# Forgetting attention with FFN: weight loading begins at the third pair, six pairs normalised behind the values

## The chip, the cores and the metric

One core of a Trainium2 chip runs the whole program in one launch. The metric is the device time of one execution in microseconds (us), the median of several runs. The engines of the core work side by side and meet at semaphores: PE (TensorE, matmuls and transposes), PEld (PE's weight loads, which overlap its matmuls), DVE (VectorE), ACT (ScalarE), POOL (GpSimd) and SP (SyncE, which issues most DMAs). Each engine takes its instructions strictly in the order in which the built program has them.

## The reference

Attention with a decay, causal, for 8 x 8 heads of 576 tokens and 64 channels, then a two-layer FFN over the 4608 tokens:

```python
scores = scale * q @ k.T                            # per head, scale = 1/8
cum = cumsum(log(clip(f, 1e-4, 1)))
scores = where(causal, -1e9, scores + cum[i] - cum[j])
attn = exp(scores - max)
attn = attn / (sum(attn) + 1e-9)
x = attn @ v                                        # heads side by side: 4608 x 512
h = x @ w_in                                        # 512 x 2048
out = maximum(0.01 * h, h) @ w_out                  # 2048 x 512
```

All inputs and outputs are fp32. The weights are handed to the kernel as the int64 words of their values and are turned into fp32 on the chip.

## The kernel before

**Accuracy.** The large matmuls run in fp32r. An operand x is split into a rounded high part and the rest, x = xh + xl, and a product is made of three matmuls: high by high, low by high, high by low. A smaller matmul may run in fp32; then one matmul of the program is two instructions on PE, except a transpose, which is one.

**The early stage.** The first 256 tokens of three batches (NE = 3) are computed by a short path, two heads (a *pair*) at a time: 12 pairs in a list `steps`. For each pair
- `early_scores` makes the scores on PE (tiles `sce`, from `qk` and from the decay in `both`), takes the row minimum on DVE (L340), the exponential and the row sum on ACT (L344), and one over the sum on DVE (L347, L348). Then the four blocks of exponentials, `ze`, are multiplied by it: on DVE (L351) in the first SCALED = 4 pairs, on ACT (L353) in the others;
- `early_values` transposes `ze` on PE (`tre`), copies the transposes on ACT (`pte`, L365), multiplies with the values on PE (`ave`, two heads into the lower and the upper 64 partitions of one tile), and evicts the result: as high and low parts `xh` (ACT, L378) and `xl` (DVE, L379) where an FFN group of 256 tokens takes it directly (batches 0 and 1), else by a copy to DRAM (L374).

**The weights.** 16 pieces of 1 MB, w_in and w_out in turn, two for each of the eight p (256 of the 2048 hidden channels). `load_weight` turns a piece into fp32 and splits it. The first SUMMED = 5 pieces let PE add up the low part (`ws`, L118; three matmuls for each of two halves, evicted at L212); the others make it on DVE alone (L195, L214, L215, L218, L219). All begin with an activation on ACT (L189) and make the high part on ACT (L200). The raw words lie in two buffers in turn (RAWS), so the load of piece n + 2 waits until piece n is turned. The first two loads are on SP's queue, the others on POOL's (L173).

**The FFN.** `ffn()` is a generator; a step of it is a *quantum*. For a group n of 256 tokens and one p it makes `h` (24 matmuls over 256 columns), g, gh and gl (ACT and DVE), and `o` (12 matmuls over 512 columns), in four quanta. The order is: group 0 and then group 1 with p = 0 to HP - 1 (HP = 4), kept as partial sums; then both with the other p; then the groups from 2 on, and two wide blocks of 512 tokens at the end. A quantum is not given out while its weights or its tokens aren't there; what the call had to spend then falls away.

**What sets the order.** Three tuples with an entry for each pair: after the scores of pair x, pieces are loaded up to the sum of WQ[:x + 1]; after the values of pair x - 1, `fill(FQ[x])` gives out that many quanta. `warm(n)` issues n matmuls on zeros, whose result isn't used, at the start (WARM[0] = 14) and behind the scores of the first pair (WARM[1] = 8). A scheduler then orders each engine's instructions; the order shown below is its result. After the 12 pairs the main stage runs 64 heads with the full-length path (`sc`, `tr`, `av`), with quanta between them, and what is left of the FFN follows.

Of the kernel before, what the change touches and what calls it, by code (L numbers as in the profile page):

```python
# [8 lines left out]
F32 = mybir.dt.float32  # L9
# [4 lines left out]
ALU = mybir.AluOpType  # L14

P = 128
DELAY = 90
ORDER = (0, 3, 4, 5, 6, 7, 1, 2)
HP = 4
PARTS = (("part0", 1), ("part1", 1), ("ost", 2), ("ost", 2))  # L20
MAXQ = 9
AT = 2
# [5 lines left out]
B2 = 5  # L28
B4 = 4
NE = 3  # L30
WQ = (1, 1, 1, 1, 1, 1, 1, 1, 2, 2, 2, 2)
ZE = (("z0", "z1", "z2", "z3"), ("e0", "e1", "e2", "e3"))
FQ = (0, 0, 0, 0, 4, 8, 8, 8, 8, 8, 8, 4, 2)
BUFS = dict(s1=2, m1=2, ost=2)
RAWS = ("ph", "pl")
WARM = (14, 8)
SCALED = 4
SUMMED = 5
NEG = -1.0e30
REBIAS = 2.0**-112  # L40
SIGN = -(2.0**32)
# [3 lines left out]
def forgetting_attention_ffn(ctx, tc, qT, kT, v4, vr, f, w_in, w_out, out):  # L45
# [6 lines left out]
    nc = tc.nc  # L52
    NHEAD, D, S = qT.shape
# [3 lines left out]
    HPB = NHEAD // NB  # L57
# [5 lines left out]
    T = 256  # L63
# [12 lines left out]
    def width(i):  # L76
        return min((i + 1) * P, S)
# [23 lines left out]
    one = ctx.enter_context(tc.tile_pool(name="one", bufs=1))  # L101
# [14 lines left out]
    def matmul(*args, **kw):  # L116
        work[0] += 1
        nc.tensor.matmul(*args, **kw)  # L118

    def transpose(*args):  # L120
        work[0] += 1
        nc.tensor.transpose(*args)  # L122
# [3 lines left out]
    def warm(n):  # L126

        ps = psum.tile([P, 512], F32, tag="h", name=f"warm_{len(warmed)}", bufs=1)
        warmed.append(n)
        for x in range(n):  # L130
            last = nc.tensor.matmul(ps, still[:, :P], still, start=True, stop=True)
            if x == 0 and len(warmed) > 1:
                tc.keep_in_program_order(last)

    warm(WARM[0])
    eye = one.tile([P, P], F32, tag="part0", name="eye")
# [3 lines left out]
    ident = ident_r.bitcast(F32)  # L140
# [36 lines left out]
    def load_weight(n):  # L177
# [12 lines left out]
        if n == 0:  # L190
            tc.keep_in_program_order(first)
        if n < SUMMED:
            first = nc.vector.tensor_scalar(t, t, 3, None, op0=ALU.logical_shift_left)
# [6 lines left out]
        nc.scalar.copy(wh, tf)  # L200
        if n < SUMMED:
            nc.vector.tensor_scalar(hi, t, -0x800000, None, op0=ALU.bitwise_and)
# [74 lines left out]
    def load(t):  # L277

        s, c0, c1 = tasks[t]
        h = state[t] = {}  # L280
        a, n = c0 * P, S
        x = h["raw"] = one.tile([P, S], F32, tag="qraw", name=f"raw_{t}")
        for y, src in ((x[:D, a:n], qT[s][:, a:n]), (x[D:, :n], kT[s][:, :n])):
            last = nc.sync.dma_start(y, src)
            if t < 2:
                tc.keep_in_program_order(last)
        if s % 2 == 0:
            pairs[s // 2, c0] = {}

    def load_v(t):  # L290

        g, o = tasks[t][0] // 2, tasks[t][0] % 2
        vm = fixed["vm"]
        for y, src in ((vm[:, :NFULL], v4[g][:, o]), (vm[:REST, NFULL], vr[g][:, o])):
            last = nc.sync.dma_start(y, src)
            if t < 1:
                tc.keep_in_program_order(last)
# [3 lines left out]
    def early_load(b, g):  # L301

        e = early[b, g] = {}
        x = e["qk"] = one.tile([P, 2, T], F32, tag="m1", name=f"qk_{b}_{g}", bufs=2)
        for y, src in enumerate((qT, kT)):
            nc.sync.dma_start(
                x[:, y], src[b * HPB + 2 * g:b * HPB + 2 * g + 2, :, :T].rearrange("s d n -> (s d) n")
            )

    def early_load_v(b, g):  # L310

        v = early[b, g]["v"] = one.tile([P, 2, T // P, D], F32, tag="b2", name=f"ve_{b}_{g}", bufs=B2)
        nc.sync.dma_start(v, v4[b * HPB // 2 + g][:, :, :T // P])

    def early_scores(b, g):
        e = early[b, g]
        mx = one.tile([P, 4], F32, tag="max", name=f"maxe_{b}_{g}", bufs=3)
        sm = one.tile([P, 4], F32, tag="sum", name=f"sume_{b}_{g}", bufs=3)
        for i in range(2):
            n = width(i)  # L320
            ps = [
                psum.tile([P, 512], F32, tag="sc", name=f"sce_{b}_{g}_{2 * o + i}")[:, :n]
                for o in range(2)
            ]
            for o in range(2):
                x = e["qk"][o * D:(o + 1) * D]
                matmul(ps[o], x[:, 0, i * P:n], x[:, 1, :n], start=True, stop=False)
            for o in range(2):
                s = b * HPB + 2 * g + o
                matmul(  # L330
                    ps[o], pick[:, s:s + 1].broadcast_to([P, P]), decay_r[i],
                    start=False, stop=True,
                )
            for o in range(2):
                c = 2 * o + i
                tag = ZE[g % 2][c]
                z = e[c] = one.tile(
                    [P, n], F32, tag=tag, name=f"ze_{b}_{g}_{c}", bufs=BUFS.get(tag, 1)
                )
                nc.vector.tensor_tensor_reduce(  # L340
                    out=z, in0=ps[o], in1=tri[:, TRI - n:], scale=-SCALE, scalar=3.0e38,
                    op0=ALU.add, op1=ALU.min, accum_out=mx[:, c:c + 1],
                )
                nc.scalar.activation(  # L344
                    z, z, AF.Exp, bias=mx[:, c:c + 1], scale=-1.0, accum_out=sm[:, c:c + 1]
                )
        nc.vector.tensor_scalar(sm, sm, 1.0e-9, None, op0=ALU.add)  # L347
        nc.vector.reciprocal(sm, sm)  # L348
        for c in range(4):
            if b * HPB // 2 + g < SCALED:  # L350
                nc.vector.tensor_scalar(e[c], e[c], sm[:, c:c + 1], None, op0=ALU.mult)  # L351
            else:
                nc.scalar.activation(e[c], e[c], AF.Copy, scale=sm[:, c:c + 1])  # L353

    def early_values(b, g):
        e = early[b, g]
        pts = []
        for o in range(2):
            ps = psum.tile([P, 512], F32, tag="tr", name=f"tre_{b}_{g}_{o}")
            for x, (c, j) in enumerate(((2 * o, 0), (2 * o + 1, 0), (2 * o + 1, 1))):  # L360
                transpose(
                    ps[:, x * P:(x + 1) * P], e[c][:, j * P:(j + 1) * P], ident
                )
            pt = one.tile([P, 3 * P], F32, tag=("z4", "e4")[o], name=f"pte_{b}_{g}_{o}")
            nc.scalar.copy(pt, ps[:, :3 * P])  # L365
            pts.append(pt)
        out = psum.tile([P, 512], F32, tag="tr", name=f"ave_{b}_{g}")
        for o, pt in enumerate(pts):
            rows_ = slice(o * D, (o + 1) * D)
            matmul(out[rows_, :T], e["v"][:, o, 0], pt[:, :T], start=True, stop=False)  # L370
            matmul(out[rows_, P:T], e["v"][:, o, 1], pt[:, T:], start=False, stop=True)
        if b not in groups:
            x = one.tile([P, T], F32, tag="x", name=f"xe_{b}_{g}")
            nc.scalar.copy(x, out[:, :T])  # L374
            nc.sync.dma_start(xd[g * P:(g + 1) * P, b * T:(b + 1) * T], x)
            return
        xh, xl = groups[b]
        nc.scalar.copy(xh[:, g, :], out[:, :T])  # L378
        nc.vector.tensor_tensor(xl[:, g, :], out[:, :T], xh[:, g, :].bitcast(F32), op=ALU.subtract)  # L379

    fixed = {}

# [231 lines left out]
    groups, staged = {}, {}  # L614
# [25 lines left out]
    def ffn():  # L640
        pending = None
        half = NFC // 2
        order = [(0, 0, HP), (1, 0, HP), (0, HP, half), (1, HP, half)]
        order += [(n, 0, half) for n in range(2, NG - 2 * WIDE)]
# [184 lines left out]
    for n in range(2):  # L829
# [8 lines left out]
        out=tri[:, TRI - P:], in_=tri[:, TRI - P:], pattern=[[-1, P]], base=0, channel_multiplier=1,  # L838
# [11 lines left out]
    for x, (b, g) in enumerate(steps + [(NE, 0)]):  # L850
        if 2 <= x + 1 < len(steps):
            early_load(*steps[x + 1])
            early_load_v(*steps[x + 1])
        if x < len(steps):
            early_scores(b, g)
            if x == 0:
                warm(WARM[1])
            if x in (8, 11):
                load(x // 11)
            if x == 8:  # L860
                load_v(0)
            if x == 10:
                split(0)
            weights(sum(WQ[:x + 1]))
        if x == 6:
            decay_rows()
        if x:
            early_values(*steps[x - 1])
            if steps[x - 1][1] == HPB // 2 - 1:
                ready[0] = (steps[x - 1][0] + 1) * T  # L870
        if x == len(steps):
            fixed["vs"] = one.tile([P, 2, NCH, 2 * D], F32R, tag="vs", name="fixed_vs")
            split_v(0)
            load_v(1)
            split(1)
        fill(FQ[x])
    fix_z()
# [73 lines left out]
```

## Time and profile before

| | |
|---|---|
| median of 3 runs | 1202.01 us (1201.11 to 1202.22) |
| the profiled execution's own time | 1203.28 us |
| its span, first to last instruction | 1201.3 us |
| PE busy | 1185.2 us, 7422 matmuls |
| DVE, ACT, POOL busy | 597.5, 630.3, 432.1 us |
| granted clock of PE, mean | 0.999 |
| read from HBM, written | 65.32 MB, 18.58 MB |

The span is a little shorter than the execution's time, since the launch lies around it. A group of instructions is named by its line in the kernel, its engine, its operation and `out<-in` with the tiles' names; the line is that of a helper where one issues them all (L118 for every matmul, L122 for every transpose). Busy time of PE is modelled: a matmul's row lasts until its end, while the next has begun long before. What a matmul costs is therefore read from where the next one starts, or from a run of several in the chain of waits. Such a run counts hardware instructions.

### The profile page before, as it was taken

To read this page: it belongs to the slowest core of one execution; us is meant where nothing else is said; L and a number is where in the kernel's file an instruction comes from. 1 tells how busy PE (TensorE), PEld (TensorE's weight loads), DVE (VectorE), ACT (ScalarE), POOL (GpSimd) and SP (SyncE) were. 2 spreads that over 40 slices of the span, in tenths; PEclk is the share of its full clock that TensorE was granted. 3 is DMA by queue.
4 is the path that set the end of the run, shared out by engine and by line. 5 is a ranking of instruction groups with operands and counts; after the bars stand their busy time and mean duration, and the time that the engine had idled before them with its cause. 6 is when DMAs were issued, how large, how long until landed. Compare 5 with 4: busy or idle time off the path is not lost.

```text
span 1201.3 us, 21523 instructions
## 1 busy us (share of the span) xinstructions
PE 1185.2 (99%) x7422; PEld 1043.4 (87%) x7422; DVE 597.5 (50%) x1695; ACT 630.3 (52%) x1629; POOL 432.1 (36%) x476
## 2 busy tenths in 40 slices
PE   8999999999999999999999999999999999999998
PEld 5777888989989899989999999999999998888886
DVE  7888365566555554455445545454435553221121
ACT  6776565677665555555555565555555652111111
POOL 3111254545554445454545444444545520000000
PEclk9999999999999999999999999999999999999999
DMA  6565233344343233333333332323232322000001
GB/s 222 172 211 167 73 102 96 100 117 119 106 143 85 78 96 104 111 81 92 109 96 90 110 97 77 111 77 94 59 104 71 88 73 77 1 1 20 16 1 36
DMA packets 81229, 110.49 MB, mean 92 GB/s; under 512 B 20640, under 2 KB 49936, under 8 KB 81120
## 3 DMA queue, kind: packets, MB, share of 16 engines
q1 hardware_dynamic: 76864, 94.16, 27.5%
q0 software_dynamic: 4032, 14.68, 3.6%
q8 instruction: 59, 0.97, 0.3%
q14 instruction: 50, 0.41, 0.1%
q10 hardware_dynamic: 224, 0.28, 0.1%
HBM read 65.32 MB, written 18.58 MB: 70 GB/s over the span
## 4 chain that ended last, share of the span: by engine, by line
PE 88%; DVE 4%; DMA 3%; ACT 2%; issue 2%; POOL 1%; SPq 0%; DVEq 0%; ACTq 0%; POOLq 0%
PE h L118 24%; PE o L118 23%; PE ow L118 7%; PE hw L118 7%; PE av L118 7%; PE tr L122 7%; PE sc L118 7%; PE sce L118 2%; PE ws L118 1%; PE ave L118 1%; DVE fixed_z L451 1%; DVE x L604 1%; DVE gh L684 1%; ACT g L681 1%; DVE pl L511 1%
## 5 line engine op out<-in xcount | busy, mean ns | idle before, releaser
L457 ACT ACTIVATE fixed_z<-fixed_z,max 128x192 f32<-128x192 f32 (+3 forms) x272 | 160.9, 592 | 101.5 <-DVE max L451 98.4
L686 POOL TENSOR_TENSOR gl<-g,gh 128x512 fp32r<-128x512 f32 x95 | 124.8, 1314 | 198.3 <-DVE gh L684 193.9
L509 ACT CAST ph<-tr 128x192 fp32r<-128x192 f32 (+3 forms) x360 | 126.0, 372 | 106.1 <-PE tr L122 74.2
L118 PE MATMUL o<-wout_h,gh 128*128 128x512 f32 x448 | 179.9, 402 | 0.3 <-ACT part L799 0.3
L118 PE MATMUL o<-wout_h,gl 128*128 128x512 f32 x448 | 176.7, 394 | 0.0
L118 PE MATMUL o<-wout_l,gh 128*128 128x512 f32 x448 | 176.5, 394 | 0.0
L451 DVE CUSTOM_DVE_ANT_0 fixed_z<-sc,tri 128x192 f32<-128x192 f32 (+3 forms) x272 | 120.9, 450 | 99.9 <-PE sc L118 98.2
L511 DVE TENSOR_TENSOR pl<-tr,ph 128x384 fp32r<-128x384 f32 (+3 forms) x296 | 136.9, 467 | 66.9 <-ACT ph L509 63.1
L118 PE MATMUL h<-xh,win_h 128*128 128x256 f32 x896 | 164.3, 287 | 0.0
L118 PE MATMUL h<-xh,win_l 128*128 128x256 f32 x896 | 159.1, 282 | 0.0
L122 PE MATMUL tr<-ident_r,fixed_z 128*128 128x128 f32 x888 | 144.0, 273 | 1.7 <-DVE x L571 1.2
L118 PEld LDWEIGHTS h<-xh,win_h 128*128 128x128 f32 x896 | 133.6, 190 | 3.9 <-issue 0.5
L118 PEld LDWEIGHTS h<-xh,win_l 128*128 128x128 f32 x896 | 129.6, 190 | 0.2
L118 PE MATMUL sc<-m,s 128*128 128x288 f32 (+1 forms) x336 | 123.0, 369 | 4.5 <-DVE max L451 4.1
L122 PEld LDWEIGHTS tr<-ident_r,fixed_z 128*128 128x128 f32 x888 | 108.0, 140 | 18.2 <-issue 1.7
L118 PE MATMUL h<-xs,win_h 128*128 128x256 f32 x768 | 123.3, 283 | 0.0
L684 DVE CAST gh<-g 128x512 fp32r<-128x512 f32 x112 | 54.3, 485 | 119.3 <-ACT g L681 113.6
L118 PEld LDWEIGHTS h<-xs,win_h 128*128 128x128 f32 x768 | 105.7, 192 | 0.0
L118 PEld LDWEIGHTS o<-wout_h,gl 128*128 128x128 f32 x448 | 84.2, 188 | 18.9 <-issue 0.2
L681 ACT ACTIVATE g<-h 128x512 f32<-128x512 f32 x112 | 66.3, 592 | 62.9 <-PE h L118 56.4
L719 ACT ACTIVATE gw<-hw 128x512 f32<-128x512 f32 x32 | 19.1, 597 | 150.9 <-PE hw L118 150.9
L118 PEld LDWEIGHTS o<-wout_h,gh 128*128 128x128 f32 x448 | 84.6, 189 | 12.8 <-ACT part L799 0.5
(152 smaller groups left out, 2151.6 us busy)
## 6 DMA issues: line engine op xcount, KB each, us to landing
raw<-in_kT SPq DMA_DIRECT2D x64, 144.0 KB
m<-m SPq DMA_DIRECT2D x64, 144.0 KB
fixed_vm<-in_v SPq DMA_DIRECT2D x64, 128.0 KB
wraw<-in_w_in POOLq DMA_DIRECT2D x14, 512.0 KB, 4.4
wraw<-in_w_out POOLq DMA_DIRECT2D x14, 512.0 KB, 4.3
xs<-xd SPq DMA_DIRECT2D x12, 512.0 KB
raw<-in_qT SPq DMA_DIRECT2D x40, 144.0 KB
s<-s SPq DMA_DIRECT2D x40, 144.0 KB
```

Source lines behind the costliest of these rows:

```text
L118: nc.tensor.matmul(*args, **kw)
L122: nc.tensor.transpose(*args)
L451: nc.vector.tensor_tensor_reduce(out=z[:, a:b], in0=ps[:m, :b - a], in1=tri[:m, at:at + b - a], scale=-SCALE, scalar=3.0e38 if x == 0 else ...
L457: nc.scalar.activation(z, z, AF.Exp, bias=h["max"][:m, last:last + 1], scale=-1.0, accum_out=fixed["sum" + "ab"[s // 2 % 2]][:m, i, s % 2: ...
L509: nc.scalar.copy(strided(ph, run), source(ps, run))
L511: nc.vector.tensor_tensor(strided(pl, run), source(ps, run), strided(ph, run).bitcast(F32), op=ALU.subtract)
L604: nc.vector.tensor_tensor(x[:, a:n], x[:, a:n], rb[:, a:n], op=ALU.mult)
L681: nc.scalar.activation(g, ph, AF.Prelu, alpha=0.01)
L684: nc.vector.tensor_copy(gh, g)
L686: eng.tensor_tensor(gl, g, gh.bitcast(F32), op=ALU.subtract)
L719: nc.scalar.activation(g, ph, AF.Prelu, alpha=0.01)
```

## The change

Weights begin at the third pair (WQ gives nothing to the first two), two pieces a pair from the fifth on, so that all 16 are given out with the eleventh pair, where it was the twelfth. FQ gives out other numbers of quanta. Group 0 and group 1 run p = 0 to 4 first (HP = 5). Six pieces instead of five are added up by PE. Behind the scores of pairs 1 to 3 stand four warm matmuls each.

In the first NORM = 6 pairs the exponentials are no longer multiplied by one over the sum. Instead PE spreads the reciprocals over the channels: four matmuls take `r` as a broadcast weight of 64 columns and the identity as the moving operand, into the free half of the `ave` tile; ACT copies them to `rb`, and DVE multiplies the values by `rb` into a new tile `x`, of which `xh` and `xl` are then made. The other six pairs are scaled on ACT.

```diff
-HP = 4
+HP = 5
...
-WQ = (1, 1, 1, 1, 1, 1, 1, 1, 2, 2, 2, 2)
+WQ = (0, 0, 1, 1, 2, 2, 2, 2, 2, 2, 2, 0)
...
-FQ = (0, 0, 0, 0, 4, 8, 8, 8, 8, 8, 8, 4, 2)
+FQ = (0, 0, 0, 0, 4, 6, 4, 4, 9, 8, 8, 4, 2)
...
-WARM = (14, 8)
-SCALED = 4
-SUMMED = 5
+WARM = (14, 8, 4, 4, 4)
+NORM = 6
+SUMMED = 6
...
+        e["r"] = sm if b * HPB // 2 + g < NORM else None
         for c in range(4):
-            if b * HPB // 2 + g < SCALED:
-                nc.vector.tensor_scalar(e[c], e[c], sm[:, c:c + 1], None, op0=ALU.mult)
-            else:
+            if e["r"] is None:
                 nc.scalar.activation(e[c], e[c], AF.Copy, scale=sm[:, c:c + 1])
...
-            pt = one.tile([P, 3 * P], F32, tag=("z4", "e4")[o], name=f"pte_{b}_{g}_{o}")
-            nc.scalar.copy(pt, ps[:, :3 * P])
+            pt = one.tile([P, 5 * P - o * T], F32, tag=("z4", "e4")[o], name=f"pte_{b}_{g}_{o}")
+            nc.scalar.copy(pt[:, :3 * P], ps[:, :3 * P])
...
+        x = out[:, :T]
+        if e["r"] is not None:
+            for c in range(4):
+                matmul(
+                    out[c // 2 * D:c // 2 * D + D, T + c % 2 * P:T + c % 2 * P + P],
+                    e["r"][:, c:c + 1].broadcast_to([P, D]), ident, start=True, stop=True,
+                )
+            rb = pts[0][:, 3 * P:]
+            nc.scalar.copy(rb, out[:, T:])
...
+        if e["r"] is not None or b not in groups:
+            x = one.tile([P, T], F32, tag="x", name=f"xe_{b}_{g}")
+            if e["r"] is None:
+                nc.scalar.copy(x, out[:, :T])
+            else:
+                nc.vector.tensor_tensor(x, out[:, :T], rb, op=ALU.mult)
...
-        nc.scalar.copy(xh[:, g, :], out[:, :T])
-        nc.vector.tensor_tensor(xl[:, g, :], out[:, :T], xh[:, g, :].bitcast(F32), op=ALU.subtract)
+        nc.scalar.copy(xh[:, g, :], x)
+        nc.vector.tensor_tensor(xl[:, g, :], x, xh[:, g, :].bitcast(F32), op=ALU.subtract)
...
-            if x == 0:
-                warm(WARM[1])
+            if x < 4:
+                warm(WARM[1 + x])
```

Where this moves instructions, at three places. The rows give the line, the operation, out<-in and the size; of the numbers in `sce_1_3` the first is the pair in its batch and the second the block, and a last, larger number only tells buffers apart.

The first place is PE during the second pair. Before:

```order
L118 MATMUL sce_1_1_271<-qk_1_182 128x256
L118 MATMUL ws_0_242<-win_l_105,ident_r 128x512
L118 MATMUL ws_1_247<-win_l_105,ident_r 128x512
L118 MATMUL sce_1_3_272<-qk_1_182 128x256
L118 MATMUL sce_1_1_271<-both 128x256
L118 MATMUL sce_1_3_272<-both 128x256
L118 MATMUL ws_0_295<-wt_289,ident_r 128x512
L118 MATMUL ws_1_300<-wt_289,ident_r 128x512
L118 MATMUL ws_0_295<-wout_h_113,minus_r 128x512
L118 MATMUL ws_1_300<-wout_h_113,minus_r 128x512
```

And on PE at the same place after the change:

```order
L118 MATMUL sce_1_1_251<-qk_1_182 128x256
L118 MATMUL sce_1_3_252<-qk_1_182 128x256
L118 MATMUL sce_1_1_251<-both 128x256
L118 MATMUL sce_1_3_252<-both 128x256
L131 MATMUL warm_265<-still 128x512 x4
L122 MATMUL tre_0_0_270<-ident_r,ze_0_1_215 128x128
L122 MATMUL tre_0_1_276<-ident_r,ze_0_2_206 128x128
L122 MATMUL tre_0_1_276<-ident_r,ze_0_3_218 128x128 x2
L118 MATMUL sce_2_0_303<-qk_2_232 128x128
L118 MATMUL sce_2_2_304<-qk_2_232 128x128
L118 MATMUL sce_2_0_303<-both 128x128
L118 MATMUL ave_0_282<-ident_r,sume_0_196 64x128 x4
```

The sums of the first two weight pieces are gone from here, the scores of the pair's two heads stand together, and four warm matmuls and the broadcasts of the first pair (`ave<-ident_r,sume`) have come.

The second place is PE where the FFN's `h` begins. Before:

```order
L118 MATMUL ws_0_520<-wt_514,ident_r 128x512
L118 MATMUL ws_1_525<-wt_514,ident_r 128x512
L118 MATMUL ws_0_520<-win_h_99,minus_r 128x512
L118 MATMUL ws_1_525<-win_h_99,minus_r 128x512
L122 MATMUL tre_3_1_536<-ident_r,ze_3_3_427 128x128
L118 MATMUL ws_0_520<-win_l_107,ident_r 128x512
L118 MATMUL ws_1_525<-win_l_107,ident_r 128x512
L118 MATMUL ave_3_542<-pte_3_0_534,ve_3_327 64x256
L118 MATMUL ave_3_542<-pte_3_0_534,ve_3_327 64x128
L118 MATMUL h_0_549<-xl_153,win_h_97 128x256
```

And on PE after the change, behind the first nine matmuls of `h_0`:

```order
L118 MATMUL h_0_553<-xl_153,win_h_97 128x256
L118 MATMUL ave_3_539<-ident_r,sume_3_382 64x128
L118 MATMUL ws_0_517<-wt_511,ident_r 128x512
L118 MATMUL ws_1_522<-wt_511,ident_r 128x512
L118 MATMUL ws_0_517<-wout_h_114,minus_r 128x512
L118 MATMUL ws_0_517<-wout_l_122,ident_r 128x512
L118 MATMUL ws_1_522<-wout_h_114,minus_r 128x512
L118 MATMUL ws_1_522<-wout_l_122,ident_r 128x512
L118 MATMUL ave_3_539<-ident_r,sume_3_382 64x128 x3
L118 MATMUL h_1_584<-xh_152,win_h_98 128x256
```

Before, five weight pieces are summed when `h` begins; now it is three, and the fourth to sixth are summed between matmuls of `h`.

The third place is DVE. Before, behind the first pair's row sums:

```order
L347 TENSOR_SCALAR sume_0_196<-sume_0_196 128x4
L348 RECIPROCAL sume_0_196<-sume_0_196 128x4
L351 TENSOR_SCALAR ze_0_0_203<-ze_0_0_203,sume_0_196 128x128
L351 TENSOR_SCALAR ze_0_1_215<-ze_0_1_215,sume_0_196 128x256
L351 TENSOR_SCALAR ze_0_2_206<-ze_0_2_206,sume_0_196 128x128
L351 TENSOR_SCALAR ze_0_3_218<-ze_0_3_218,sume_0_196 128x256
L193 TENSOR_SCALAR wt_236<-wt_236 128x1024
L340 ISA ze_1_0_265,maxe_1_257<-sce_1_0_259,tri 128x128
L340 ISA maxe_1_257 128x1
L202 TENSOR_SCALAR wraw_185<-wt_236 128x1024
```

After the change, DVE in the third pair:

```order
L385 TENSOR_TENSOR xe_0_292<-ave_0_282,pte_0_0_274 128x256
L340 ISA ze_2_3_324,maxe_2_301<-sce_2_3_316,tri 128x256
L340 ISA maxe_2_301 128x1
L391 TENSOR_TENSOR xl_153<-xe_0_292,xh_152 128x256
L347 TENSOR_SCALAR sume_2_302<-sume_2_302 128x4
L348 RECIPROCAL sume_2_302<-sume_2_302 128x4
L193 TENSOR_SCALAR wt_334<-wt_334 128x1024
L340 ISA ze_3_0_389,maxe_3_381<-sce_3_0_383,tri 128x128
L340 ISA maxe_3_381 128x1
L202 TENSOR_SCALAR wraw_185<-wt_334 128x1024
```

The four scalings at L351 are gone, the product with the broadcast reciprocals (L385) has come, and the first weight piece (L193) now stands behind the third pair's row sums instead of the first's.

More of the change, by code (lines that the diff above doesn't have):

```diff
@@ L370, in early_values @@
             matmul(out[rows_, :T], e["v"][:, o, 0], pt[:, :T], start=True, stop=False)
-            matmul(out[rows_, P:T], e["v"][:, o, 1], pt[:, T:], start=False, stop=True)
+            matmul(out[rows_, P:T], e["v"][:, o, 1], pt[:, T:3 * P], start=False, stop=True)
+        if e["r"] is not None or b not in groups:
[4 more added lines that the diff above has]
+                nc.vector.tensor_tensor(x, out[:, :T], rb, op=ALU.mult)
         if b not in groups:
-            x = one.tile([P, T], F32, tag="x", name=f"xe_{b}_{g}")
-            nc.scalar.copy(x, out[:, :T])
             nc.sync.dma_start(xd[g * P:(g + 1) * P, b * T:(b + 1) * T], x)
```

## The prediction

> **What bounds the kernel now.** I read the page first, then the table of stretches, then who waits for whom on PE, then the chain of waits in order of time.
>
> ```profile
> span 1201.3 us, 21523 instructions
> PE 1185.2 (99%) x7422; PEld 1043.4 (87%) x7422; DVE 597.5 (50%) x1695; ACT 630.3 (52%) x1629; POOL 432.1 (36%) x476
> PE 88%; DVE 4%; DMA 3%; ACT 2%; issue 2%; POOL 1%; SPq 0%; DVEq 0%; ACTq 0%; POOLq 0%
> ```
>
> PE (TensorE) is busy 99% of the span and holds 88% of the chain. A share of busy time is not a share of useful time, so the stretches come next: start and end, length, then busy time and instructions of PE, PEld, DVE, ACT and POOL, the granted clock, the DMA share and GB/s. 43.26 is where the FFN begins in earnest, 143.40 where the main attention stage begins.
>
> ```profile
> 0.00:14.00 14.00, 10.94 (x47) 7.85 (x47) 9.73 (x31) 7.38 (x17) 6.36 (x19) 1.00 0.81 260
> 14.00:43.26 29.26, 28.78 (x131) 15.66 (x131) 24.88 (x75) 23.82 (x57) 6.13 (x10) 1.00 0.58 192
> 43.26:63.00 19.74, 19.74 (x127) 16.16 (x128) 17.14 (x38) 14.28 (x31) 2.37 (x4) 1.00 0.54 185
> 63.00:97.00 34.00, 33.77 (x204) 25.48 (x204) 29.05 (x69) 25.94 (x65) 4.31 (x8) 1.00 0.56 186
> 97.00:143.40 46.40, 45.26 (x286) 37.61 (x285) 27.55 (x56) 28.18 (x62) 9.89 (x16) 1.00 0.35 108
> 143.40:420.00 276.60, 271.28 (x1836) 247.45 (x1836) 158.96 (x480) 174.15 (x474) 135.66 (x146) 1.00 0.38 107
> 420.00:980.00 560.00, 559.13 (x3798) 515.25 (x3797) 277.35 (x850) 320.39 (x858) 265.96 (x273) 1.00 0.33 93
> ```
>
> Between 14 and 143.4 us PE lacks 0.48 + 0 + 0.23 + 1.14 = 1.85 us of being always busy; in the first 14 us it lacks 3.06 us. DVE and ACT are over 80% busy from 14 to 43 us, yet PE hides it. The waits of PE up to 144 us, and the longest one behind it (total, times, longest), say the same:
>
> ```profile
> PE sce L118 <- DVE maxe L340: 2.0, 4, 1.0
> PE warm L131 <- DVE tables L111: 1.5, 1, 1.5
> PE sc L118 <- DVE max L451: 4.1, 10, 0.7
> ```
>
> So PE's work sets the time, also in the stage that the change rewrites. Whatever the change puts on PE counts, unless it falls into these few microseconds of waiting; what it takes from DVE and ACT counts only through them.
>
> **Part 1, work added to PE.** Counted in the order of instructions of both kernels, three kinds are new on PE and none is gone: 12 warm matmuls (34 for 22), 24 broadcast matmuls (one a 64x128 block of reciprocals, six pairs of four), and one more weight piece added up on PE. The prices, from the timeline of PE and the chain of waits (start, length, what, how many hardware instructions; an fp32 matmul counts two, a transpose one):
>
> ```profile
> 1.46 5.28 PE L131 MATMUL warm<-still 128*128 128x512 f32 x14 [1.46 <-DVE tables L111]
> ...
> 9.04 0.91 PE L118 MATMUL sce<-qk 64*128 64x256 f32 x4 [1.00 <-DVE maxe L340]
> ...
> 10.21 2.01 PE L131 MATMUL warm<-still 128*128 128x512 f32 x8
> ```
> ```profile
> 20.95 0.81 PE ave L118 x8
> 21.76 0.41 PE sce L118 x2
> ...
> 26.29 2.18 PE ws L118 x6
> 28.48 0.57 PE ave L118 x2
> 29.05 0.67 PE ws L118 x2
> 29.71 0.80 PE ave L118 x5
> ...
> 42.53 0.79 PE ave L118 x4
> ```
>
> Warm: 2.01/8 = 0.25 us each, 12 make 3.0 us. Weight piece: 2.18 + 0.67 = 2.85 us. The trace has no broadcast matmul; the nearest row is an ave half, also fp32 into 64 partitions: 0.79 us for four instructions over 256, 256, 128 and 128 columns, 768 in all. A pair's four broadcasts are eight instructions over 128 columns, 1024, so 0.79 x 1024/768 = 1.05 us if they run one after the other. The 0.81 us row shows both halves of an ave side by side in the time of one, which would make 0.53 us. Upward, one fp32 matmul of 128 columns that stands alone (the sce x2 row) takes 0.41 us; the 24 stand at ten places, so ten at 0.41 and fourteen at 1.05/4 make 7.8 us. Bounds 3.2 to 7.8 us; the order has two of the same half in succession, so little can overlap, and I take 5.5 us, near the ave row. Sum: 3.0 + 2.85 + 5.5 = 11.35 us.
>
> [...]
>
> **Part 2, what goes.** (a) The ave matmuls of pairs 1 to 3 stand cut up by weight sums now (0.57 and 0.80, together 1.37 us); in the changed order those of pairs 0 to 5 stand together. If both halves are ready, 1.37 - 0.81 = 0.56 us goes for five of them, 2.8 us; if their evictions come one by one, nothing. I take 2.0. (b) Waits: of the 1.85 us I take 1.0. (c) Warm matmuls hidden in waits: without weight sums PE must wait somewhere in pairs 1 to 3, as the 8 warm ones stand in a wait now; one group of four, 1.0 us. Together 4.0 us.
>
> **Part 3, off PE.** DVE loses the 16 scalings of pairs 0 to 3, ACT the 8 of pairs 4 and 5; each of six pairs gains one product of 128x256 on DVE and one copy on ACT.
>
> ```profile
> L351 DVE TENSOR_SCALAR ze<-ze,sume 128x256 f32<-128x256 f32 x8 | 2.8, 351 | 0.0
> L351 DVE TENSOR_SCALAR ze<-ze,sume 128x128 f32<-128x128 f32 x8 | 2.3, 283 | 0.1
> L379 DVE TENSOR_TENSOR xl<-ave,xh 128x256 fp32r<-128x256 f32 x3 | 1.3, 421 | 1.0 <-ACT xh L378 1.0
> ```
>
> That is 2.8 + 2.3 - 6 x 0.42 = 2.6 us less on DVE, all beside a busy PE: nothing. The product is a new wait (values, product, then xh and xl) behind which the next exponentials queue on ACT; PE has scores and sums to do meanwhile, and if that cover is gone it costs about 0.42 us a pair. No DMA is added: the first two weight loads stay at their place on SP's queue, the other fourteen keep POOL's, which does nothing else here. They start when the raw buffer is free.
>
> **Part 4, what is moved.** The start of the FFN first.
>
> ```profile
> 43.33 1.99 PE h L118 x15
> ...
> 57.31 2.87 PE h L118 x24
> 60.18 2.77 PE o L118 x12
> ```
> ```profile
> 143.44 0.31 PE L118 MATMUL sc<-m,s 128*128 128x320 f32 x1
> ```
>
> In front of h PE does two pieces less now (5.7 us), 12 broadcasts (2.75) and 12 warm matmuls (3.0) more, and with half of Part 2 (2.0) h comes at 43.3 - 5.7 + 5.75 - 2.0 = 41 us. It hardly comes earlier. Up to the main stage's first scores PE did 288 h and 126 o matmuls; now 312 and 138. That is 24 x 2.87/24 + 12 x 2.77/12 = 5.6 us done ahead instead of later, on a PE that is full in both places: nothing. The stage's end itself moves from 143.4 to about 143.4 + 5.6 + 7.35 = 156 us. HP and the numbers of quanta change no count.
>
> **The sum.** 11.35 - 4.0 = 7.35 us more. Against the profiled execution (span 1201.3, its own time 1203.28, 1.98 us around it) that is 1210.6 us; it lies 1.27 us above the median of the runs, 1202.01, and the prediction is for the median: **1209.4 us**. With every unknown at its ends: 0 + 2.85 + 3.2 - 2.8 - 1.85 = +1.4 us, and 3.0 + 2.85 + 7.8 + 2 us of new waits = +15.6 us. About 0.2% (2.4 us) is what a measurement of this kernel can tell from no change.
>
> **Rivals.** *The FFN starts early (faster).* Four pairs without weights leave DVE and ACT free, the group of tokens is ready early, and PE gets h sooner. The end follows the start of h one to one. Behind it PE has 143.4 - 43.3 = 100.1 us now, plus three pieces (8.55), 12 broadcasts (2.75), 5.6 us of FFN, less 2.0: 115.0 us, of which 5.6 come back. So it decides at 143.4 + 5.6 - 115.0 = 34 us: with h at 31 us the kernel takes 1199 us. For it: DVE and ACT are 85% and 81% busy there. Against it: PE's own work fills the time to 41 us, or 38 us with all 12 warm ones hidden. Chance 0.15. *It evens out.* Warm matmuls hidden, halves overlapping, all ave together, waits gone: the lower end, +1.4 us, 1203.4 us; chance 0.2. *The weights come late (more slower).* After h begins, 13 pieces are still to convert, not 11:
>
> ```profile
> L195 DVE TENSOR_SCALAR wt<-wt 128x1024 int32<-128x1024 int32 x11 | 7.8, 708 | 5.0 <-ACT wt L189 4.8
> L214 DVE TENSOR_SCALAR wraw<-wraw 128x1024 int32<-128x1024 int32 x11 | 7.6, 689 | 0.0
> L215 DVE SCALAR_TENSOR_TENSOR wraw<-wraw 128x1024 int32<-128x1024 int32 x11 | 13.5, 1228 | 0.3
> L218 DVE TENSOR_SCALAR wraw<-wt 128x1024 int32<-128x1024 int32 x11 | 7.6, 693 | 0.1
> L219 DVE SCALAR_TENSOR_TENSOR win_l<-wraw 128x1024 fp32r<-128x1024 int32 x5 | 6.1, 1222 | 0.1
> ```
>
> A piece takes 0.71 + 0.69 + 1.23 + 0.69 + 1.22 = 4.5 us of DVE, two a pair 9 us, and between 63 and 97 us DVE has only 34 - 29.05 = 5 us free. One piece too many there stalls h by 4.5 us: 1213.9 us. For it: pairs 6 and 7 give PE only four quanta each. Against it: PE is by then behind by the sums of pairs 4 and 5. Chance 0.2. The forecast keeps 0.45, from 1205 to 1213 us.
>
> **Range and chances.** Faster by over 0.2% 0.15, within 0.2% 0.2, slower 0.65. The range leaves out about a tenth at each end: 1199.5 to 1214.0 us.
>
> **What will show it.** PE's busy time up by about 9 to 11 us with waits hardly less; the first long run of h at 38 to 43 us, not at 31; the main stage's first scores near 156 us (149 is where nothing changes); a pair's four broadcasts at 0.53 to 1.3 us; ave x8 at 0.81 in pairs 1 to 5; from 420 us on, stretches as full as before. Wrong if h begins at 34 us or earlier, or if PE shows waits of over 1 us on win_l or wout_l behind 60 us.

## The result, and the profile after

The changed kernel takes **1217.75 us** (median of 4 runs, 1217.25 to 1218.9), the kernel before 1202.11 us beside it: a ratio of 1.0131, 95% interval 1.012 to 1.0143, so 15.6 us slower. The forecast was 7.35 us slower, with a range that ended at 1214.0 us. The profiled execution took 1218.9 us, its span grew from 1201.3 to 1217.0 us. One execution among the experiments below, of run 15, came at a mean granted clock of 0.85 and took 1280.65 us; its ratio leaves it out.

From the page of the changed kernel, the busy times:

```profile
span 1217.0 us, 21659 instructions
...
PE 1198.3 (98%) x7490; PEld 1051.5 (86%) x7490; DVE 596.1 (49%) x1685; ACT 630.8 (52%) x1628; POOL 432.1 (36%) x475
```

PE is busy 13.1 us longer, where 9 to 11 us were expected, and its waits grew by 2.6 us. The table of stretches (columns as in the prediction) shows where. 39.86 is where the run of `h` begins (43.26 before, forecast 41), 161.06 where the main stage's first scores stand (143.44 before; 149 would have been no change, forecast 156):

```profile
14.00:39.86 25.86, 25.48 (x145) 16.26 (x145) 16.82 (x52) 19.30 (x52) 3.35 (x6) 1.00 0.44 142
39.86:63.00 23.14, 23.09 (x138) 16.19 (x138) 15.32 (x32) 15.44 (x28) 3.19 (x6) 1.00 0.47 163
63.00:97.00 34.00, 33.39 (x201) 24.62 (x198) 29.74 (x70) 23.02 (x55) 5.58 (x8) 1.00 0.59 191
97.00:126.00 29.00, 29.00 (x191) 25.14 (x191) 25.18 (x44) 18.05 (x36) 4.95 (x8) 1.00 0.56 181
126.00:135.00 9.00, 7.16 (x25) 4.42 (x24) 5.47 (x13) 4.21 (x10) 0.00 (x0) 0.64 0.06 16
...
161.06:426.00 264.94, 257.50 (x1747) 234.75 (x1746) 154.08 (x472) 168.78 (x463) 130.06 (x139) 1.00 0.39 109
426.00:986.00 560.00, 559.44 (x3787) 513.74 (x3786) 278.55 (x845) 320.61 (x856) 269.72 (x275) 1.00 0.33 93
```

Two rows are new. From 126 to 135 us PE stands for 1.84 us, and the granted clock is 0.64, where before no stretch fell below 1.00: at that clock 9 us do the work of 5.8, so 3.2 us are lost (between 132 and 135 us `h` matmuls in a row start 0.21 us apart, against 0.12 us ahead of the wait). This is the profiled execution, whose mean granted clock is 0.997. The other three (1217.25 to 1217.92 us) have 0.999 (0.9985 at the least), so 0.0015 x 1217 = 1.8 us at most can have been lost in them. And in the main stage up to 426 us PE lacks 7.4 us of being busy, against 5.3 us before. The waits of PE up to 165 us (first row) and behind it say who is waited for:

```profile
PE sce L118 <- DVE maxe L340: 2.9, 2, 1.8
```
```profile
PE sc L118 <- DVE max L463: 4.2, 8, 0.9
PE tr L122 <- DVE x L583: 1.6, 1, 1.6
PE tr L122 <- POOL fixed_z L475: 1.1, 1, 1.1
```

The chain of waits of the changed kernel tells how the first of them comes about (start, length, what):

```profile
120.95 5.08 DMA wraw<-in_w_out
126.02 0.02 issue
126.04 0.04 ACTq L189
126.08 0.04 issue
126.13 1.13 ACT wt L189
127.26 0.02 issue
127.28 0.04 DVE wt L195
127.32 0.57 issue
127.89 0.28 DVE ze L340
128.17 0.02 DVE maxe L340
128.19 0.04 issue
128.24 2.10 PE sce L118 x6
```

The sixteenth weight piece is loaded, for 5.08 us, into a buffer that has only just come free. Its conversion on ACT waits for the load, its shift on DVE (L195) for ACT, and behind that shift, in DVE's queue, stands the score reduction (L340) of pair 10, for which PE's next scores wait. PE wants no weight here; it waits for the queue in which the weight stands.

To compare stages in which different numbers of quanta are done, I use a **ledger**: of each PE matmul the time from its start to the next one's start, the waits apart, summed by kind from the records of both traces. Of each stage's time 0.120 us for every `h` matmul and 0.231 us for every `o` matmul are then taken off (2.87/24 and 2.77/12, from the prediction's rows), so that FFN work done ahead counts for nothing. What is left changes so:

| stage | before, us | after, us | difference |
|---|---|---|---|
| first matmul to the main stage's first scores | 78.32 | 90.28 | +11.96 |
| the next 200 score matmuls | 92.10 | 94.81 | +2.71 |
| the rest | 391.0 | 392.1 | +1.1 |

| kind, early stage | matmuls before, after | before, us | after, us | difference | forecast |
|---|---|---|---|---|---|
| warm | 22, 34 | 7.15 | 10.02 | +2.87 | +3.0, of it 1.0 hidden |
| broadcasts | 0, 48 | 0 | 5.62 | +5.62 | +5.5 |
| weight sums | 40, 48 | 14.59 | 16.32 | +1.72 | +2.85 |
| ave | 96, 96 | 16.00 | 14.12 | -1.88 | -2.0 |
| transposes | 72, 72 | 9.09 | 8.01 | -1.08 | 0 |
| scores | 144, 144 | 24.46 | 25.83 | +1.37 | 0 |
| h and o, less the quanta done ahead | | 3.58 | 6.10 | +2.53 | 0 |
| waits | | 3.45 | 4.27 | +0.82 | -1.0 |

The priced work comes to 2.87 + 5.62 + 1.72 - 1.88 - 1.08 = 7.25 us; the forecast's terms for it, without waits and hiding, make 9.35 us. Missed are the waits, the slower scores and FFN matmuls (in this execution the lowered clock, 3.2 us from 126 to 135 us, for a good part), and 3.8 us of a main stage that was to pay nothing. Whether such a ledger also says what a part of the change *costs* is for the experiments.

### The profile page after: what moved, and what is told of

Same layout as the page of the kernel before. It is cut to its first block, busy times and chain, and to the rows that moved or that the text cites. A ratio compares the mean times of both kernels' runs of the same rounds, so it can differ in the third digit from the quotient of the medians.

```text
span 1217.0 us, 21659 instructions
## 1 busy us (share of the span) xinstructions
PE 1198.3 (98%) x7490; PEld 1051.5 (86%) x7490; DVE 596.1 (49%) x1685; ACT 630.8 (52%) x1628; POOL 432.1 (36%) x475
## 4 chain that ended last, share of the span: by engine, by line
PE 83%; DVE 3%; ACT 2%; DMA 1%; issue 1%; POOL 1%; SPq 0%; POOLq 0%; ACTq 0%; DVEq 0%
PE h L118 23%; PE o L118 22%; PE av L118 7%; PE ow L118 7%; PE hw L118 7%; PE tr L122 7%; PE sc L118 7%; DVE fixed_z L463 1%; DVE x L616 1%; ACT g L693 1%; DVE gh L696 1%; PE ave L118 0%; DMA wraw<-in_w_out 0%; DMA raw<-in_qT 0%; DVE pl L523 0%
## 5 line engine op out<-in xcount | busy, mean ns | idle before, releaser
L118 PEld LDWEIGHTS o<-wout_l,gh 128*128 128x128 f32 x448 | 84.5, 189 | 12.3 <-issue 0.2
```

## The experiments

The first theory, the forecast's own, is **added work**: the loss is what was put on PE. The rival is **order**: the pieces and quanta stand in places where PE waits, and the work would have cost little elsewhere. Each kernel was timed beside the kernel before on the same chip. "Rest" is the ledger's difference against before in the early stage, the next 200 scores, and behind, in the one profiled execution. It adds up to that execution's time and not to the median: the profiled execution of run 2 took 1211.58 us, that of run 15 1209.05 us, both over their medians.

| run | median, us | before beside it | ratio, 95% interval | rest: early, 200 scores, behind |
|---|---|---|---|---|
| the change | 1217.75 | 1202.11 | 1.0131 (1.012 to 1.0143) | 12.0, 2.7, 1.1 |
| 1 tables alone | 1207.44 | 1202.41 | 1.0049 (1.0037 to 1.0061) | 0.0, 2.2, 0.9 |
| 2 tables undone | 1208.13 | 1202.41 | 1.0056 (1.0044 to 1.0068) | 7.3, 0.7, 0.2 |
| 3 without the 12 warm | 1223.27 | 1202.41 | 1.0164 (1.0146 to 1.0183) | 16.9, 2.6, 1.2 |
| 4 normalisation undone | 1219.59 | 1202.41 | 1.0144 (1.0131 to 1.0157) | 9.1, 5.0, 1.2 |
| 5 last piece a pair later | 1217.17 | 1201.53 | 1.012 (1.0105 to 1.0135) | 10.0, 3.0, 1.1 |
| 6 45 quanta ahead | 1216.7 | 1201.53 | 1.0127 (1.0114 to 1.014) | 11.4, 4.1, 0.0 |
| 7 tables alone, 45 ahead | 1207.33 | 1201.53 | 1.0048 (1.0032 to 1.0063) | 1.9, 1.4, 0.0 |
| 8 five sums | 1211.26 | 1201.53 | 1.0084 (1.0071 to 1.0097) | 4.4, 2.0, 1.1 |
| 9 piece behind the scores | 1214.6 | 1202.61 | 1.0102 (1.0089 to 1.0115) | 9.2, 2.5, 1.2 |
| 10 the same, HP = 4 | 1214.49 | 1202.61 | 1.0102 (1.0089 to 1.0115) | 13.6, -0.1, 0.3 |
| 11 broadcasts alone | 1203.08 | 1202.61 | 1.0003 (0.9994 to 1.0011) | 3.5, -0.9, 0.1 |
| 12 sixth sum alone | 1202.85 | 1202.61 | 1.0008 (0.9999 to 1.0016) | 0.8, -1.7, 0.0 |
| 13 warm alone | 1202.94 | 1202.57 | 1.0002 (0.9993 to 1.001) | 0.7, -1.6, 0.8 |
| 14 9 with HP = 4, five sums | 1209.13 | 1202.57 | 1.0055 (1.004 to 1.007) | 4.4, 3.4, 0.1 |
| 15 tables alone, HP = 4 | 1207.02 | 1202.57 | 1.0033 (1.0021 to 1.0045) | 5.6, 0.3, 0.1 |

**1 and 2: the tables alone, and the change without them.** In the kernel before

```diff
-HP = 4
+HP = 5
-WQ = (1, 1, 1, 1, 1, 1, 1, 1, 2, 2, 2, 2)
+WQ = (0, 0, 1, 1, 2, 2, 2, 2, 2, 2, 2, 0)
-FQ = (0, 0, 0, 0, 4, 8, 8, 8, 8, 8, 8, 4, 2)
+FQ = (0, 0, 0, 0, 4, 6, 4, 4, 9, 8, 8, 4, 2)
```

and the reverse of it in the changed one.

> The kernel before with the three tables of the change alone (when weight pieces are converted, how many FFN quanta follow each pair, how many pieces lie in the first part): no broadcasts, no more warm matmuls, five pieces summed on TensorE. Added-work theory (the loss is the work added to TensorE, the order is worth a little): ave stands together, -2 us against before, so 1200 to 1202 us. Order theory (pieces in pairs of two come late, the scores wait behind them, the clock falls, the main stage inherits the lag): about 4 to 8 us slower than before, 1206 to 1210 us, with a wait of scores on the row maxima of over 1 us between 110 and 140 us.

> The changed kernel with the three tables of before; broadcasts, 12 warm matmuls and the sixth summed piece stay. Added-work theory: all of 2.9 (warm) + 5.6 (broadcasts) + 1.7 to 2.9 (sums) stays, ave is cut up again (+2): 1212 to 1218 us. Order theory: the wait of 2 us and the half-speed clock behind it go, and so does the 3.8 us of the main stage, 1209 to 1212 us, with main-stage waits as before.

The tables alone lose 5.0 us without one more matmul on PE; by added work they were to gain 2. The wait came too, but as 1.22 us at 103 us, and the clock stayed at 1.00 in the profiled execution. The sixteenth piece has no part in it: here the reductions of pair 10 stand ahead of that piece on DVE, and PE shows no wait from 106 to 149 us. Taken out of the changed kernel they give back 9.9 us (15.6 - 5.7), more than the order theory asked for, though a wait of 1.93 us stays, with a stretch of clock 0.71 behind it. The main stage's loss goes with the tables: 2.2 us with them alone, 0.7 us without them.

**3 and 4: the added warm matmuls and the broadcasts taken out.** For 3, in the changed kernel

```diff
-WARM = (14, 8, 4, 4, 4)
+WARM = (14, 8)
-            if x < 4:
-                warm(WARM[1 + x])
+            if x == 0:
+                warm(WARM[1])
```

and for 4 the scalings of before come back (NORM = 0; DVE in the first four pairs, ACT in the others).

> The changed kernel without the 12 added warm matmuls. If they lie in the way (forecast 3.0 us, 2.9 us in the trace): 1214.5 to 1215 us. If they only fill waits: no change, 1217 to 1218 us. If they save a fall of the clock in pairs 1 to 3: 1219 us or more, with a granted clock under 1.0 between 14 and 40 us.

> The changed kernel with the normalisation of before (16 scalings on DVE, the rest on ACT, no broadcasts, no product behind the values). Added-work theory: the 24 broadcasts are 5.6 us on TensorE, so 1212 us. Cover theory: without them TensorE waits for DVE and ACT in pairs 0 to 4, where no weight sums fill the time, and 2 to 4 us of it come back as waits: 1214 to 1216 us.

Both parts had the largest prices of the forecast, and taking either out makes the kernel no faster. Without the warm matmuls it is 5.2 us slower (20.9 against 15.6). Without the broadcasts it is 1.5 us slower (17.2 against 15.6), which the two intervals don't tell from no change. In 3 the third of the named cases came true. The timeline of PE shows a wait for the load of the keys where a warm group stood, and four stretches show what came behind it (the granted clock is the third number from the end):

```profile
16.81 0.51 PE L118 MATMUL sce<-qk 64*128 64x128 f32 x2 [1.74 <-DMA qk<-in_kT]
```
```profile
12.00:16.00 4.00, 3.03 (x20) 1.95 (x18) 1.53 (x10) 2.04 (x8) 0.00 (x0) 1.00 0.86 254
16.00:20.00 4.00, 3.19 (x16) 2.25 (x16) 0.63 (x5) 1.10 (x5) 0.00 (x0) 0.64 0.07 25
20.00:24.00 4.00, 4.00 (x13) 2.00 (x14) 0.54 (x3) 1.22 (x5) 0.00 (x0) 0.50 0.00 0
24.00:28.00 4.00, 4.00 (x21) 2.97 (x20) 1.28 (x6) 3.01 (x8) 0.00 (x0) 0.58 0.36 102
```

Work lost to the clock: (0.36 + 0.50 + 0.42) x 4 = 5.1 us, about the whole difference. Three of the four executions of run 3 show it (mean clock 0.992 to 0.993); the fourth, at 0.999, took 1216.95 us, no more than the change. As far as that one execution tells, the warm matmuls cost next to nothing, and what they save is the clock. In 4 both expectations were missed. Without broadcasts PE has 5.6 us less to do early, but `ave` takes 17.4 us instead of 14.1, and the next 200 scores lose 5.0 us instead of 2.7, of it 4.1 in waits instead of 2.0.

**5 and 9: the wait at 126 us.** For 5 WQ ends in 2, 1, 1 instead of 2, 2, 0; for 9

```diff
-FQ = (0, 0, 0, 0, 4, 6, 4, 4, 9, 8, 8, 4, 2)
+FQ = (0, 0, 0, 0, 4, 6, 4, 4, 8, 8, 9, 4, 2)
```

> The changed kernel with the sixteenth weight piece converted a pair later (last numbers of the table of pieces 2, 1, 1 instead of 2, 2, 0). Theory of the raw buffer: the piece's load can start only when the piece before has freed its buffer, and the scores of pair 10 stand behind it on DVE; with a pair between, the wait of 1.8 us at 126 us and the half-speed clock behind it (0.64 over 9 us, 3.2 us lost in the profiled run) go: 1213 to 1215.5 us, granted clock 1.00 between 126 and 140 us. Rival (the wait only moves to the next pair, and with it the clock): 1217 to 1219 us.

> The changed kernel with one quantum of the FFN moved from pair 8 to pair 10 (8, 8, 9 for 9, 8, 8): the same work, but DVE's instructions for the sixteenth piece now stand behind the score reductions of pair 10 instead of ahead of them. Theory of the queue (the scores wait behind a piece whose load lands late): the wait of 1.8 us at 126 us goes, and the 3.2 us of lowered clock behind it: 1213 to 1215 us. Rival (the time is work on TensorE, and the wait is made up for elsewhere): 1217 to 1218 us.

Run 5 decides nothing on the theory, since it didn't do what it was to do: the scheduler put the sixteenth piece at the same place of DVE's queue, ahead of pair 10's reductions, and the wait stayed (2.04 us). Run 9 has the same work and a different order there. DVE's timeline in it (start, length, line, operation):

```profile
126.56 0.28 DVE L340 CUSTOM_DVE_ANT_0 ze<-sce,tri 128x128 f32<-128x128 f32 x1
...
128.52 0.42 DVE L340 CUSTOM_DVE_ANT_0 ze<-sce,tri 128x256 f32<-128x256 f32 x1
128.86 0.08 DVE L340 DVE_READ_ACCUMULATOR2_ANT maxe<- 128x1 f32 x1
128.86 0.69 DVE L195 TENSOR_SCALAR wt<-wt 128x1024 int32<-128x1024 int32 x1
```

The reductions now come first, and the shift of the piece (L195) behind them. Two stretches of this run, to be read against the 126 to 135 us of the change:

```profile
125.00:130.00 5.00, 3.69 (x27) 2.82 (x24) 5.00 (x15) 2.72 (x8) 0.00 (x0) 1.00 0.35 116
130.00:135.00 5.00, 5.00 (x34) 4.37 (x33) 3.41 (x6) 4.01 (x11) 0.00 (x0) 1.00 0.09 30
```

The clock stays at 1.00; a wait of 0.92 us is left. The span is 2.9 us shorter than that of the change, the time 3.6 us nearer to before (12.0 for 15.6). PE's instructions are the same in both kernels and in the same order, but for 141 of 7490 between 108 and 134 us. Where the orders part, run 9 stands 1.0 us behind the change, and where they meet again 2.25 us ahead. So it is shown that the order at this place costs about 3 us, and the rival that the time is work falls for this part. In the profiled executions the lowered clock (3.4 us) makes nearly all of it; PE's early waits differ by only 0.34 us. What the other executions of the change pay there is not shown, since at 0.999 they can have lost 1.8 us at most and are still about 3 us slower than those of run 9.

**6, 7, 10 and 15: what lies ahead of the main stage.** 6 and 7 ask for 6, 2 instead of 8, 4 quanta at pairs 10 and 11; 10 and 15 set HP = 4 (46 quanta ahead instead of 49).

> The changed kernel with 45 quanta of the FFN asked for ahead of the main stage instead of 49 (8, 4 at pairs 10 and 11 made 6, 2). Theory that quanta done ahead are missing as cover later: the waits of the transposes at the beginning of the main stage (1.64 and 1.13 us) shrink to those of before (about 0.5 us each): 2 us less, 1215 to 1216 us. Rival, as in the prediction (ahead or later is all the same): 1217 to 1218 us, waits as they were.

> The three tables alone in the kernel before (the first run of this study), with 45 quanta asked for ahead instead of 49. Cover theory: its loss of 2.2 us in the first part of the main stage goes, and it comes to 1203 to 1204.5 us in undisturbed executions, against 1206 with 49. Rival (ahead or later is all the same): 1206 us.

> The run before with the first part of the FFN at four pieces as before instead of five (46 quanta lie ahead of the main stage, not 49). Theory that the parts of five leave the first tasks of the main stage without cover: its waits of transposes (1.6 and 1.1 us) shrink to 0.5 us each and 2 to 3 us go against the run before. Rival: the waits of the main stage come from the loads of the heads, and stay: the same time as the run before within 0.7 us.

> The kernel before with the tables of pieces and quanta of the change, but the first part of the FFN at four pieces as before. If the parts of five make the loss of the tables (2.2 us in the first 200 scores and 1.1 us behind): 1203 to 1204.5 us, against 1206 to 1207.5 with five. If the weights that begin at the third pair make it: 1206 us or more.

No total moved as the theory of missing cover (a quantum done ahead no longer covers a wait later) said: 6 against the change, 7 and 15 against 1, and 10 against 9 are all within 0.8 us, each against its own runs of before. But the ledger shows that the loss moved. In 10 the waits of the main stage's beginning shrink as expected (PE's waits from 158 to 376 us in 10, then in 9):

```profile
PE sc L118 <- DVE max L463: 3.2, 7, 0.9
PE tr L122 <- DVE ph L528: 0.4, 1, 0.4
PE tr L122 <- DVE x L583: 0.4, 1, 0.4
PE tr L122 <- POOL fixed_z L475: 0.2, 1, 0.2
```
```profile
PE sc L118 <- DVE max L463: 3.3, 6, 0.9
PE tr L122 <- DVE x L583: 1.7, 1, 1.7
PE tr L122 <- POOL fixed_z L475: 1.3, 1, 1.3
```

The next 200 scores and what lies behind them are 3.4 us shorter than in 9 (2.5 + 1.2 against -0.1 + 0.3), and the early stage is 4.4 us longer: with fewer quanta PE waits 1.50 us at 97 us, and the clock falls behind it (3.4 of the 4.4 us). The other executions of run 10 (1213.78 to 1214.49 us) have a clock of 0.999 or 1.0 and are hardly faster than those of run 9, so this trace doesn't tell what takes the gain back in them.

```profile
96.00:100.00 4.00, 2.50 (x12) 1.41 (x10) 3.57 (x9) 3.28 (x10) 0.00 (x0) 0.83 0.32 119
100.00:104.00 4.00, 4.00 (x18) 3.69 (x18) 3.21 (x8) 2.84 (x8) 1.07 (x2) 0.50 0.27 69
104.00:108.00 4.00, 4.00 (x22) 3.40 (x22) 2.77 (x4) 2.03 (x4) 0.00 (x0) 0.82 0.50 194
```

The tables alone read the same way: 0.0 early and 3.1 behind with 49 quanta, 1.9 and 1.4 with 45, 5.6 and 0.4 with parts of four (1.7 us of the 5.6 in a clock fall). In 6 the 1.1 us behind the first 200 scores go too, and those scores lose 1.4 us more, with a clock fall of 1.7 us among them. A quantum that covers an early wait is missing where a later one is covered. That is how these runs read; no run shows it for a single quantum. Nor does the number alone decide: 6, 7, 10 and 15 all have 288 `h` and 132 `o` matmuls ahead of the main stage's first scores, and 7 and 15 divide their loss differently.

Run 15 came out as its second case, 1206 us or more, and run 7 is no faster than run 1. So neither HP nor the quanta of pairs 10 and 11 make the 5.0 us of the tables. The late beginning of the weights (WQ) and the other numbers in FQ remain, and were not tried apart.

**8 and 14: the sixth sum, and three remedies together.** 8 sets SUMMED = 5 in the changed kernel; 14 adds to it the table of 9 and HP = 4.

> The changed kernel with five pieces added up on TensorE instead of six. Forecast's price: 2.9 us less, 1214.7 us; by the trace's ledger (ws 16.3 against 14.6 us) 1.7 us less, 1215.9 us. Rival: the sixth piece then takes DVE 2.6 us longer (L214 and L215, 0.69 + 1.23, and L219 at 1.22 instead of a copy of about 0.6) and the scores wait for it: 1217 us or more.

> The changed kernel with the piece behind the scores (quanta 8, 8, 9), the first part of the FFN at four pieces and five sums on TensorE. If the remedies add up (3.5 for the wait and the clock, 3.6 for the main stage, 2.9 for the sum): 15.6 - 10 = 5.6 us above before, 1207 to 1209 us, with no wait over 1.2 us and no fall of the clock. If a new wait takes the place of each: 1211 us or more, as with five sums alone.

Five sums give back 5.9 us (9.7 for 15.6), twice the forecast's price and against the direction of the rival. The sums (`ws`) are 2.9 us shorter, and the scheduler, with other lengths before it, now puts pair 10's reductions ahead of the last piece, as in 9, so the wait and the low clock go too (the longest wait of scores on `maxe` is 0.7 us, the clock 1.00 up to 200 us). All three together reach 6.6 us above before, one more than the sum of the remedies foresaw, with a new wait of 2.25 us at 253 us and the clock at 0.63 from 256 to 260 us behind it in the profiled execution; the single executions lie at 1206.9 to 1207.2 us or at 1211.0 to 1211.5 us, and the median between the two.

**11, 12 and 13: each addition alone.** The kernel before with one part of the change, its own tables kept.

> The kernel before with the broadcasts and the product behind the values for six pairs, and nothing else of the change (tables, sums and warm matmuls of before). Forecast's price: 5.5 us less what comes of whole ave and transposes (-2 to -3.5): 1204 to 1206 us. By the ledger of the run with the tables undone (broadcasts 3.9, ave -2.5, transposes -1.1): +0.4 us, 1202 to 1203 us. Rival (DVE and ACT set the pace of the first pairs, and are relieved): 1198 to 1201 us.

> The kernel before with the sixth piece added up on TensorE and nothing else of the change. Forecast's price 2.85 us: 1204.5 us. By the ledger 1.3 to 1.7 us: 1203.3 us. If DVE's 2.6 us less a piece shorten a wait: 1201 to 1202 us. If the 6.3 us that the sum costs in the changed kernel are its own: 1208 us.

> The kernel before with the 12 warm matmuls added behind the scores of pairs 1 to 3, nothing else. Forecast's price, 3.0 us with one group hidden: +2 to +3 us, 1204 to 1205.5 us. If weight sums and FFN leave no wait there: +3 us. If warm matmuls prevent a fall of the clock that before has in some executions: 1201 to 1202 us.

24 broadcasts cost 0.5 us, the sum 0.2 us, 12 warm matmuls 0.4 us, none of them to be told from no change, against 5.5, 2.85 and 3.0 in the forecast. The warm ones are the plainest: they take 3.03 us more on PE, and the early waits shrink by 0.98 us, the scores by 1.18 us, the waits among the next 200 scores by 1.17 us. In those two stages together the rest is 0.9 us shorter (0.7 - 1.6). The 3.5 us early in run 11 hold a clock fall of 3.4 us, which not every execution had. In all three runs the first 200 scores give back 0.9 to 1.7 us, mostly in waits, as if what PE waits for there were not late with it; that reason was not tried by itself. The absorption has an end, however: all three in the old tables (run 2) cost 5.7 us.

No version beat the kernel before.

## Why the prediction was wrong

The direction was right and the mechanism named for it wrong in half. The steps, in the forecast's order:

- **PE bounds, so "whatever the change puts on PE counts".** Too strong. 3 us put on PE alone cost 0.4 us (run 13). A stage that is 97 to 100% busy still has waits that move: the 4.8 us in the first 200 scores of before were counted as idle of another stage and left out, and they are where additions vanish.
- **Part 1.** The sizes on PE were near for the warm matmuls and the broadcasts (2.87 for 3.0, 5.62 for 5.5) and too high for the sum (1.72 for 2.85). As prices they were not: alone 0.4, 0.5 and 0.2 us in that order, and taken out of the changed kernel +1.5 (broadcasts, not clear of noise), -5.9 (sum) and +5.2 us (warm). The forecast gave the 12 warm matmuls a price and nothing in return; that was the author's assumption, and wrong: without them the clock fell to 0.50 behind a wait of 1.74 us and 5.1 us were lost (run 3).
- **Part 2.** (a) held: -1.88 for -2.0, and the transposes gained another 1.08 us. (b) and (c), waits and hidden warm matmuls worth -2.0, didn't come; the early waits grew by 0.82 us.
- **Part 3** is not contradicted: run 11, which takes the scalings from DVE, gains nothing.
- **Part 4 is the step that failed:** "5.6 us done ahead instead of later, on a PE that is full in both places: nothing. ... HP and the numbers of quanta change no count." The count is the same, the place is not. The tables cost 5.0 us alone and 9.9 us in the changed kernel; with them undone, everything else costs 5.7 us (run 2), less than the 7.35 forecast for the whole. Of the 9.9 us about 3 us are the order at one place, the sixteenth piece ahead of pair 10's scores (run 9). The main stage's beginning and what lies behind it make 3.4 us in run 10's trace, which the early stage then takes back. Which table makes the 5.0 us is open, but it is not HP (run 15).
- **The rivals.** "The FFN starts early" was told from the forecast by the start of `h`, 39.9 us, as it said. "The weights come late" named the cause, a piece that is converted too late, but priced a stall of `h` on DVE at 63 to 97 us. It came at 126 us, through the queue ahead of the scores, and behind the wait of 1.84 us the clock stood at 0.64 over 9 us in the profiled execution. It was to be known by a wait on win_l or wout_l; the wait is on `maxe`, so that sign would have missed it.
- **The range** ended at 12 us of loss. The outer sum of the working, 15.6 us, happens to equal the measured loss but is made of other terms. New waits had been given 2 us at most, without a row for it, and the clock no price at all.

What stays open: the three additions cost 1.1 us one by one and 5.7 us together (run 2), the tables 5.0 us, and all of it 15.6 us. About 3 us of the 4.9 us left over are likely what run 9 gives back, since PE has no such wait in run 1 and only 0.8 us behind that piece in run 2; no run shows it directly. The rest is not assigned; the scheduler orders every engine anew in each kernel, and no run held all queues but one fixed.

## What to carry to other kernels

Before pricing work on the busiest engine, find the waits behind it that don't move with it: here three additions cost 1.1 us one by one, while such waits shrank beside them, and 5.7 us together. For work that is moved, count what it covered where it was and who stands behind it in each engine's queue: here a load of 5.08 us into a buffer that came free late held up scores that have nothing to do with it, and PE waited 1.84 us. Where a table of numbers feeds a scheduler, look at the order that comes out for the one or two instructions that decide, and at the granted clock behind each wait. Compare the mean clock of the profiled execution with that of the others before reading a loss off its trace: here it was the one execution of four in which the clock fell that far.

## What the runs showed of the hardware

Within the first 280 us the granted clock fell in eight of the fifteen experiments' profiled executions and in that of the change, but not in that of before. The lost work, summed over stretches of 4 us as above:

| run | PE's last wait ahead of it, us | lost, us |
|---|---|---|
| the change, 126 us | 1.84 | 3.4 |
| 2, 117 us | 1.93 | 1.7 |
| 3, 15 us and 131 us | 1.74 and 2.78 | 5.1 and 3.4 |
| 5, 127 us | 2.04 | 1.7 |
| 6, 126 us and 183 us | 1.48, and 2.40 in all from 180 to 188 us | 3.4 and 1.7 |
| 10, 97 us | 1.50 | 3.4 |
| 11, 96 us | 1.09 | 3.4 |
| 14, 253 us | 2.25 | 1.7 |
| 15, 89 us | 0.65 | 1.7 |

The lowest clock of any of these stretches is 0.50 (run 3 from 20 to 24 us, run 10 from 100 to 104 us); in the change every stretch of 1 us from 129 to 135 us has it, and the next has 0.82. At 0.50 the losses of the table stand for about 3.4 to 10.2 us of lowered clock, an estimate from its last column, and no wait was as long as the fall behind it. The length of the wait doesn't decide alone. PE lacked 1.67 us of being busy from 176 to 180 us and 1.95 us from 208 to 212 us in run 4, 1.68 us from 176 to 180 us in run 9 and 2.26 us from 172 to 180 us in run 7, and the clock stayed at 1.00 there and in the stretches behind. In run 15 it fell behind a wait of 0.65 us, in a stretch of short fp32 matmuls with a wait of 0.24 us just ahead. What else decides is not shown.

Not every execution of a kernel is hit alike: the tables alone ran 1205.9 us at a mean clock of 0.999 and 1210.7 us at 0.997.
